# Attention with a position bias, then a gated FFN, on one core: another fixed issue order per engine

## The chip, the cores and the metric

One Trainium2 chip, of which the kernel uses one core. The metric is the device time of one execution in microseconds (us); the kernel before has a median of 652.33 us.

## The reference

The FFN's input is the attention's output; q, k and v are 4 x 8 x 576 x 64, w_in is 512 x 2048 and w_out 2048 x 512.

```python
def _attn_ref(q, k, v, w1, b1, w2):
    scores = scale * np.matmul(q, k.transpose(0, 1, 3, 2))
    rel = (pos[:, None] - pos[None, :]).astype(np.float32)
    psi_rel = np.log1p(np.abs(rel))
    psi_i = np.log1p(np.maximum(pos[:, None].astype(np.float32), 1.0))
    x = (psi_rel / psi_i)[..., None]
    h = np.maximum(x @ w1 + b1, 0.0)
    bias = h @ w2
    scores = scores + bias.transpose(2, 0, 1)[None, :, :, :]
    scores = scores - np.max(scores, axis=-1, keepdims=True)
    attn = np.exp(scores)
    attn = attn / (np.sum(attn, axis=-1, keepdims=True) + 1e-09)
    return np.matmul(attn, v).astype(np.float32)
...
x = np.ascontiguousarray(attn_out.transpose(0, 2, 1, 3)).reshape(B * S, H * D)
...
def _moe_ref(x, w_in, w_out):
    h = x @ w_in
    relu6 = np.clip(h + 3.0, 0.0, 6.0)
    g = h * relu6 / 6.0
    return (g @ w_out).astype(np.float32)
```

## The kernel before

**The bias table.** All heads and batches share one table of distances T. 36 groups of 16 positions are made. For a group, VectorE (DVE) or ScalarE (ACT) computes hidden units z (L1016, L1020; tiles `z_e` and `z_a`, used in turn), and TensorE (PE) multiplies them with w2 (`b_ps`: L1058 for the first 16 groups, L1037 for the later ones, which are written `bias_far`). ACT evicts (`bo`, L1076), and the table goes to HBM, from where later stages read it (`bias`, tile `bt`).

**The start.** DVE scales T by w1 in two halves (L1244: 636 columns, then 512), prepares b1 and w2 (L1247 to L1249) and clears a part of `z_a` (L1252), from which PE runs eight products of nothing but zeros (`w_ps`, L1255). Four small products `c_ps` (L1258) give the constant part of the bias, copied out at L1267.

**Attention** goes by units of two heads and a query tile. Scores `s_ps` are direct fp32 products for the first units (L683, with filler products of T before them, L680) and sums of three split products later (L703, of `qkh` from ACT, L557, and `qkl` from GpSimd, POOL, L564). DVE adds the bias and takes the maximum (L715), ACT takes exp (L726). The first units are transposed on PE (`t_ps`, L778 and L781) and evicted by ACT (`atf`, L784); the later ones are split into halves (`hl`, ACT L285 and DVE L302) and turned by a DMA (`at<-hl`). Products with V are `pv_ps` (L822, L833, L868).

**The FFN** takes blocks of 256 or 320 tokens: `h_ps` (L937) from `x` and `wi`, the gate on ACT (L927, L914), DVE (L920) and POOL (L916), then `o_ps` (L960) from `g` and `wo`; ACT evicts `ot` (L970). Before the first block its weights are split into high and low halves (L396 to L420, DVE L414, L417, L420, ACT L406), and DVE scales x (L1342, in `open_ffn`).

**Tile sizes on PE.** A product uses a part of the 128 x 128 array: h_ps, o_ps, t_ps and w_ps use 128*128 (rows * columns), b_ps and c_ps 128*32, s_ps 64*128 (one kind 128*128), pv_ps 128*64 or 64*64. Below, a switch is a matmul pass that has another tile size than the pass ahead of it on PE.

**The order.** The program is traced once. Then `ISSUE`, a table of numbers per engine (L36 on), gives the order in which each engine issues its instructions: the numbers are places in the traced sequence, and each instruction is made to follow the one before it in the list. After the end of a list the traced order goes on. The DMA queues of SP and POOL are in the table too.

```python
for name, seq in traced.items():
    order = []
    for run in ISSUE[name].split():
        lo, _, hi = run.partition("-")
        order.extend(range(int(lo), int(hi or lo) + 1))
    order.extend(range(len(order), len(seq)))
    for a, b in zip(order, order[1:]):
        tc.add_manual_dep(seq[b], seq[a].name, after, reason="order")
```

An engine so stands still at an instruction whose input is late, even if a later one in its list could run.

Of the kernel before, what the change touches and what calls it, by code (L numbers as in the profile page):

```python
# [37 lines left out]
0-1 3 2 23 4 6 15 18 5 20 7 10 8 22 25 11-12 9 13-14 17 31 16 19 21 26 24 27-28 30 33 29 32 38 34 47  # L38
36-37 35 51 54 40 48 39 43 59 42 50 57 55 52 41 60 44 49 45 62 46 63 56 53 58 65 67 69 68 64 61 66
76 70 75 73-74 78 77 80 79 71 83-84 82 72 81 86 85 87 89 91 90 94 92 99 88 97 95 101 93 98 96 102  # L40
100 103 109 108 106-107 112 111 110 113 104 114 117 105 121 116 120 119 122 124 118 115 130 123 132
127-129 134 133 135 131 126 125
""",
    "Pool": """
2-9 15 19 12 10 13 21 11 22 14 23 25-26 17 16 27 24 20 30 35 29 28 33 36 34 31 37 40 38-39 44 41 18
45 48 42 46-47 49 43 32 53 51 0 52 62 54 57 50 63 58 56 60 59 61 55 64 74 66 65 67-68 75 69 72 70-71
73 1 76 78 77 81 93 82 92 79-80 83-84 87 85 88 86 89 96 90-91 94 102-105 95 97-101 106-111 113-114
116-118 112 115 119 126-127 129-130 120-123 131 124-125 128 132 138-141 133-136 142 137 143-147
149-150 152-154 148 151 155 162-163 165-166 156-159 167 160-161 164 168 174-177 169-172 178 173
179-183 185-186 188-190 184 187 191 198-199 201-202 192-195 203 196-197 200 204 210-213 205-208 214  # L50
209 215-219 221-222 224-226 220 223 227 234-235 237-238 228-231 239 232-233 236 240-244 246 245
""",
    "Activation": """
0-1 3-4 7-8 5 12 11 6 9 15 13 16 19 2 14 20 17 24 21 28 10 18 22 25 29 26 32 36 27 37 23 33 30 41-42
31 34 38 46 45 40 35 39 43 50 58 44 47 52 51 59 55 74 54 62 48 56 61 65 53 66 63 57 49 67 64 70 68
75 71 60 80 72 69 73 81 77 76 84 78-79 82 86 88 83 90 85 87 89 92-94 96 99 91 102 95 97 101 100 108
104 103 106 109 107 111 113 110 137 146 112 114 117-118 105 98 115 119 121 116 120 123 151 125 122
124 126-127 129 132 152 128 173 131 157 134 130 139 142 140 138 147 158 165 135 141 133 148 153 144
136 166 149 154 174 159 145 160-161 175 167 162 168 201 155 143 150 163 176 169 180 186 177 181 156
192 188 182-183 187 164 189 205 171-172 193 184 178 194-195 206 179 190 216 202 196 198 207 185 191  # L60
204 199 218 208 219-221 213 215 222 214 223-224 217 203 200 225 170 209 226 238 232 210 233 211 231
227-228 197 229 234 212 244 266 264 235 230 236 241 258 242 280 250 237 243 247-248 239 274 253
256-257 240 254 245 259 265 246 249 260 293 262 255 263 251 272 267-268 261 270 269 271 273 276 275
281 285 278 277 282-283 291 279 284 286 292 252 290 302 294 297 287 295 304 298 289 296 288 303
305-306 300 313 307 323 299 336 301 309 308 310 312 311 314-315 319-321 318 324 322 330 316 329 333
325 334 331 317 326 328 332 345 327 343 335 340 350 341 337-338 342 347 339 346 355-356 351 344 361
352-353 357 354 358-359 365 348 372 349 367 374 366 368 371 360 369 394 362 370 364 382 389 363 379
373 375 377 376 383 378 384 390 386 392 380 406 388 385 381 393 391 395 408 397 396 399 407 387 432
398 400 423 409 401 411 417 410 418 402-403 424 404 413 405 415 414 416 420-421 425 419 430 437 422
431 412 427 426 438-439 433 429 428 434-435 440 459 444 467-468 436 450 445 441-442 451 443 446-448  # L70
457 452 449 462 458 453-454 463-464 456 455 476 465 484-485 471 466 460 472 461 474 479 475 469 480
470 481 473 482 486 483 477 487 478 496 507-508 489-490 494 502 500 488 495 501 491-493 497-498 503
505 499 513 506 504 509 514 510 526 511 518 512 538-539 515 519-520 524 516 531 533 517 522 525 532
521 523 528 527 529 534 536 530 544 537 535 540 545 541 557 542 549 543 565-566 546 550-551 555 547
560 562 548 553 556 561 552 554 563 567 564 558 568 559 576 584-585 572-574 579 581 575 571 580
569-570 582 586 583 577 587 578 596 607-608 589-590 594 600 602 588 595 601 591-593 598 597 603 605
613 599 606 614 604 609-610 626 611 615 638-639 618 612 619-620 616 624 631 633 622 625 617 632 621
623 627-629 634 636 644 630 637 645 635 640-641 657 642 646 665-666 649 643 650-651 647 655 660 662
653 656 648 661 652 654 663 667 664 668 658-659 676 684-685 672-674 679 681 675 671 680 669-670 682
686 683 687 677-678 696 707-708 689-690 694 700 702 688 695 701 691-693 698 697 703 705 713 699 706  # L80
# [12 lines left out]
68 60 58 63 61 70-71 73-74 72 75 67 82-84 87-88 91 79-80 92-93 89 85 94 109-110 90 96 122 100 81 104
97-99 101 108 119 102-103 123 105 112 115-116 113 117 114 121 126 125 129 118 127 133 124 106 128
131 107 132 111 137 143 120 130 153 138 135 144 139 172 175-177 173-174 136 134 141 149 180 142 155
150 148 146 183 147 145 140 313 154 152 184-185 163-164 181-182 151 188 191 160 158 189-190 165 157
166 156 161 167 192-193 162 159 200 203 199 178 201 168 204 169 186 202 170 205 179 210 213 197 194
209 214 195 198 187 215 211 206 216 222 212 223 225 207 226 196 227 224 230 218-219 221 208 231 451
228 233 239 232 217 234-235 171 236 245 237 220 248 238 249 269 259 251 246 229 241 252 240 242 247
258 243 253-254 257 256 261-262 274 273 293 275 263 284 260 266-268 277 276 265 278 281 270 250 279  # L100
244 289 255 280 264 286 272 296 285 294 282 287-288 283 297-298 290 314 291-292 316 315 330 306 308
295 299 326 317 302 301 300 320 335 305 307 304 309 318 303 311-312 331 319 310 327 336 328 324 321
323 329 325 322 332 338 342-343 339 334 346 333 341 350 348-349 344 337 347 360 354 340 355 345 356
351 361 359 357 368 365 362 352 364 372 358 453 369 371 363 379 366-367 370 376 378 387 375 271 377
# [1399 lines left out]
```

## Time and profile before

| what | before |
|---|---|
| time, three runs | 654.21, 652.02, 652.33 us; median 652.33 us |
| the profiled execution, its time and its span | 653.62 us, 651.5 us |
| granted clock of TensorE in it, as a share of full speed | 0.995 |
| TensorE busy | 625.5 us, 96% of the span, 5440 matmul passes |
| VectorE, ScalarE, GpSimd busy | 459.8, 504.7, 208.3 us |

The time of an execution is its span and 2.1 us around it. Busy times count an engine's instructions, without waits.

### The profile page before, as it was taken

How to read it: one execution, taken by the hardware profiler on the slowest of the kernel's cores; microseconds unless marked ns; L12 is line 12 of the kernel's file. 1: busy time of each engine (PE TensorE's matmuls, PEld its weight loads, DVE VectorE, ACT ScalarE, POOL GpSimd, SP SyncE). 2: the span in 40 equal slices, each digit the busy share in tenths (PEclk: the TensorE clock that was granted, in tenths of full speed). 3: DMA queues.
4: the chain of work that ended last, by engine and by line, in shares of the span. 5: the costliest groups of instructions: out<-in, count | busy, mean ns of one | idle time of the engine just before them, and what ended most of it. 6: DMA issues, size and time to landing. Idle time of an engine off the chain costs nothing.

```text
span 651.5 us, 14774 instructions
## 1 busy us (share of the span) xinstructions
PE 625.5 (96%) x5440; PEld 447.9 (69%) x5440; DVE 459.8 (71%) x1116; ACT 504.7 (77%) x993; POOL 208.3 (32%) x267
## 2 busy tenths in 40 slices
PE   6688998999999999999999999999999999999997
PEld 2225655666777777788888877777777777777775
DVE  4899999999858887676788667776677667821310
ACT  5898887999979989896799778976797678822620
POOL 0111115664223430452255125521444026300410
PEclk9889999999999999999999999999999999999999
DMA  8888788864679999999999999889878877640000
GB/s 278 317 322 298 283 310 318 308 232 140 163 205 247 215 274 194 264 251 234 257 259 248 203 209 180 176 177 205 173 142 187 181 168 139 113 81 21 1 12 31
DMA packets 176648, 130.57 MB, mean 200 GB/s; under 512 B 138304, under 2 KB 145728, under 8 KB 175552
## 3 DMA queue, kind: packets, MB, share of 16 engines
q1 hardware_dynamic: 166784, 114.14, 70.9%
q10 hardware_dynamic: 9792, 15.49, 8.5%
q8 instruction: 43, 0.70, 0.5%
q14 instruction: 29, 0.24, 0.1%
HBM read 77.54 MB, written 15.49 MB: 143 GB/s over the span
## 4 chain that ended last, share of the span: by engine, by line
PE 71%; DVE 4%; DMA 3%; ACT 1%; issue 0%; ACTq 0%; DVEq 0%; SPq 0%
PE o_ps L960 27%; PE h_ps L937 26%; PE s_ps L703 9%; PE pv_ps L868 6%; DMA at<-hl 2%; PE b_ps L1037 2%; DVE bt L715 1%; DMA wo<-in_w_out_dram 1%; DVE cu L420 1%; DVE cu L414 1%; ACT bt L726 0%; DVE wo L302 0%; PE pv_ps L822 0%; DVE cu L417 0%; ACT hl L285 0%
## 5 line engine op out<-in xcount | busy, mean ns | idle before, releaser
L937 PE MATMUL h_ps<-x,wi 128*128 128x256 f16 (+1 forms) x1536 | 205.7, 286 | 1.2 <-DVE x L1342 0.8
L960 PE MATMUL o_ps<-g,wo 128*128 128x256 f16 (+1 forms) x1536 | 198.8, 286 | 0.0
L937 PEld LDWEIGHTS <-wi 128*128 128x128 f16 x1536 | 146.6, 98 | 52.1 <-issue 15.8
L960 PEld LDWEIGHTS <-wo 128*128 128x128 f16 x1536 | 146.8, 98 | 46.4 <-issue 9.6
L916 POOL TENSOR_TENSOR g<-t,g 128x256 f16<-128x256 f32 (+1 forms) x128 | 105.0, 832 | 180.9 <-ACT g L914 173.9
L726 ACT ACTIVATE bt<-bt,sm 128x576 f32<-128x576 f32 x144 | 110.7, 770 | 31.0 <-DVE sm L715 30.6
L302 DVE SCALAR_TENSOR_TENSOR hl<-bt,sm,hl 128x576 f16<-128x576 f32 x112 | 95.2, 864 | 16.5 <-ACT hl L285 15.0
L285 ACT ACTIVATE hl<-bt,sm 128x576 f16<-128x576 f32 x112 | 84.0, 765 | 5.3 <-ACT bt L726 3.3
L920 DVE SCALAR_TENSOR_TENSOR t<-t,t,h_ps 128x320 f32<-128x320 f32 (+1 forms) x112 | 57.2, 516 | 40.2 <-ACT t L927 39.3
L564 POOL TENSOR_TENSOR qkl<-st,qkh 128x576 fp32r<-128x576 f32 (+2 forms) x48 | 53.1, 1124 | 90.3 <-ACT qkh L557 59.0
L914 ACT ACTIVATE g<-t 128x256 f16<-128x256 f32 (+1 forms) x128 | 54.9, 438 | 22.7 <-DVE t L920 22.3
L927 ACT ACTIVATE t<-h_ps,t,hr 128x320 f32<-128x320 f32 (+1 forms) x112 | 64.6, 586 | 8.4 <-PE h_ps L937 6.9
L715 DVE CUSTOM_DVE_ANT_0 bt<-s_ps,bt 128x576 f32<-128x576 f32 x88 | 64.8, 750 | 4.6 <-PE s_ps L703 4.4
L1016 DVE TENSOR_SCALAR z_e<-T,nbp 128x576 f32<-128x576 f32 (+17 forms) x76 | 36.5, 498 | 16.8 <-PE b_ps L1037 12.0
L734 DVE TENSOR_SCALAR sm<-sm 128x1 f32<-128x1 f32 x112 | 16.9, 151 | 44.0 <-ACT bt L726 43.7
L970 ACT ACTIVATE ot<-o_ps,os 128x256 f32<-128x256 f32 (+1 forms) x32 | 15.7, 491 | 38.4 <-PE o_ps L960 37.7
L1076 ACT ACTIVATE bo<-b_ps,cv_sb,isc 128x576 f32<-128x576 f32 (+36 forms) x60 | 36.7, 635 | 1.5 <-PE b_ps L1037 1.1
L715 DVE CUSTOM_DVE_ANT_0 bt<-s_ps,k 128x576 f32<-128x576 f32 x40 | 28.8, 752 | 5.9 <-PE s_ps L703 5.6
L407 POOL TENSOR_SCALAR w<-w 128x1024 f32<-128x1024 f32 x8 | 10.5, 1315 | 68.1 <-ACT wo L406 68.1
L868 PE MATMUL pv_ps<-at,vh 128*64 128x320 f16 (+1 forms) x432 | 32.0, 293 | 0.0
L1020 ACT ACTIVATE z_e<-T,bp 128x576 f32<-128x576 f32 (+17 forms) x36 | 24.9, 698 | 8.2 <-DVE bp L1247 3.4
L781 PE MATMUL t_ps<-eye_sb,bt 128*128 128x128 f32 x160 | 29.3, 280 | 1.1 <-ACT atf L784 0.5
(130 smaller groups left out, 845.0 us busy)
## 6 DMA issues: line engine op xcount, KB each, us to landing
bt<-bias SPq DMA_DIRECT2D x36, 576.0 KB, 5.6
w<-in_w_in_dram SPq DMA_DIRECT2D x8, 1024.0 KB, 6.6
vs<-in_vp_dram SPq DMA_DIRECT2D x24, 320.0 KB, 4.1
st<-in_qk_dram SPq DMA_DIRECT2D x16, 448.0 KB, 4.3
bias<-bo ACTq DMA_DIRECT2D x20, 295.5 KB, 4.4
wo<-in_w_out_dram SPq DMA_DIRECT2D x5, 1024.0 KB, 4.8
bias<-bo ACTq DMA_DIRECT2D x16, 288.0 KB, 4.3
bt<-bias SPq DMA_DIRECT2D x32, 144.0 KB, 3.3
```

What stands on the lines that cost most here:

```text
L285: nc.scalar.activation(out=out, in_=full, func=AF.Copy, scale=scale)
L302: nc.vector.scalar_tensor_tensor(out=out, in0=full, scalar=scale, in1=high, op0=ALU.mult, op1=ALU.subtract)
L703: nc.tensor.matmul(out=s_t[n + j][:, a, 0:HALF], lhsT=w[q], rhs=m[rows, cs], start=(k == 0), stop=(k == 2),)
L715: nc.vector.tensor_tensor_reduce(out=halves(bt), in0=ps, in1=halves(src), op0=ALU.add, op1=ALU.min, scale=-0.125, scalar=3.0e38, accum_out ...
L726: nc.scalar.activation(out=bt, in_=bt, func=AF.Exp, scale=-1.0, bias=sm[:, 0:1], accum_out=total)
L868: nc.tensor.matmul(out=ps[64 * s:64 * s + 64, 0:n], lhsT=w[:, 128 * c + 64 * s:128 * c + 64 * s + 64], rhs=at[:, c, s * n:(s + 1) * n], st ...
L914: nc.scalar.activation(out=g[:, 0], in_=uu, func=AF.Copy)
L916: e.tensor_sub(out=g[:, 1], in0=uu, in1=g[:, 0])
L920: nc.vector.scalar_tensor_tensor(out=t_t[f], in0=t_t[f], scalar=cols(f)[2], in1=h_t.pop(f)[:, 0:n], op0=ALU.min, op1=ALU.mult,)
L927: nc.scalar.activation(out=t_t[f], in_=h_t[f][:, 0:n], func=AF.Relu, scale=cols(f)[0], bias=cols(f)[1],)
L937: nc.tensor.matmul(out=h_t[f][:, 0:n], lhsT=wi[:, a, c, f * 128:(f + 1) * 128], rhs=x[:, e, c], start=(k == 0), stop=(k == 3 * KC - 1),)
L960: nc.tensor.matmul(out=ops[:, 0:n], lhsT=wo[:, a, f, e * 128:(e + 1) * 128], rhs=g_t[f][:, r], start=(f == 0 and a == 0 and r == 0), stop= ...
```

## The change

Only the table `ISSUE` differs: the products of PE, and the instructions of the other four engines' lists, are in another order. What is computed, the tiles and the buffers are the same. The table is 13 lines longer, so all lines after it stand 13 further down (L937 is L950).

```diff
 ISSUE = {
     "SP": """
-0-1 3 2 23 4 6 15 18 5 20 7 10 8 22 25 11-12 9 13-14 17 31 16 19 21 26 24 27-28 30 33 29 32 38 34 47
...
+0-1 3 2 7 4 15 18 6 20 5 8 22 10 23 25 11-12 9 14 13 17 31 16 19 21 26 24 27-28 33 30 29 47 32 34 36
...
```

Counted in the two orders, PE makes 276 switches before and 245 after. The places are given by the time at which the pass stands in the trace of before:

| stretch of the trace of before | switches before | after |
|---|---|---|
| up to the first h_ps (109.93 us) | 70 | 60 |
| from there to 302 us | 123 | 102 |
| 302 us to the end | 83 | 83 |

Of the 21 fewer after 109.93 us, 11 stand ahead of 160 us and 10 behind. From 302 us on PE's order is the same word for word; those of the other engines are the same or differ in which statistic is written first.

The first place is the start of PE's program. Before, `c_ps` stands between the products of zeros and ahead of the bias products `b_ps`:

```order
L1255 LDWEIGHTS z_a
L1255 MATMUL w_ps<-z_a 128x512
L1258 MATMUL c_ps<-b_sb,w_sb 32x1 x2
L1255 LDWEIGHTS z_a
L1255 MATMUL w_ps<-z_a 128x512
L1258 MATMUL c_ps<-b_sb,w_sb 32x1
L1058 MATMUL b_ps<-z_e,w_sb 32x288 x6
```

After, at the same place (the lines are L1268, L1271 and L1071 now):

```order
L1268 LDWEIGHTS z_a
L1268 MATMUL w_ps<-z_a 128x512
L1071 MATMUL b_ps<-z_e,w_sb 32x288
L1071 MATMUL b_ps<-z_a,w_sb 32x288
L1071 MATMUL b_ps<-z_e,w_sb 32x288 x3
L1271 MATMUL c_ps<-b_sb,w_sb 32x1
L1071 MATMUL b_ps<-z_e,w_sb 32x288 x2
L1271 MATMUL c_ps<-b_sb,w_sb 32x1 x2
```

The products of zeros are one run now, and the `c_ps` products stand among the `b_ps` products, which have their tile size.

The second place is the start of DVE's program, before:

```order
L1244 TENSOR_SCALAR T<-T,w_sb 128x636
L1240 MEMSET c_120 128x1
L1252 MEMSET z_a 128x576
L1247 TENSOR_SCALAR bp<-bp,b_sb 128x144
L1248 TENSOR_SCALAR nbp<-bp 128x144
L1016 TENSOR_SCALAR z_e<-T,nbp 128x576
L1016 TENSOR_SCALAR z_a<-T,nbp 128x576 x2
L1249 TENSOR_SCALAR w_sb<-w_sb 128x32
L1016 TENSOR_SCALAR z_e<-T,nbp 128x576 x2
L1238 MEMSET cv_sb 128x2
L1267 COPY cv_sb<-c_ps 32x1 x2
```

and after:

```order
L1265 MEMSET z_a 128x576
L1257 TENSOR_SCALAR T<-T,w_sb 128x636
L1253 MEMSET c_120 128x1
L1260 TENSOR_SCALAR bp<-bp,b_sb 128x144
L1261 TENSOR_SCALAR nbp<-bp 128x144
L1029 TENSOR_SCALAR z_a<-T,nbp 128x576
L1251 MEMSET cv_sb 128x2
L1029 TENSOR_SCALAR z_e<-T,nbp 128x576
L1262 TENSOR_SCALAR w_sb<-w_sb 128x32
L1029 TENSOR_SCALAR z_e<-T,nbp 128x576
L1029 TENSOR_SCALAR z_a<-T,nbp 128x576
L349 TENSOR_REDUCE vparts<-vf 128x1
```

The clearing of `z_a` is DVE's first instruction now, and one `z` fewer stands ahead of the scaling of w2. A reduction of V (L336, now L349) follows the fourth `z`, then comes the second half of T, and behind it the next `z_e` and the copies of `c_ps`. SP's list has the DMA of T's second half as its fifth and no longer as its twelfth.

The third place is on PE, where a unit of two scores is moved (with buffer numbers). Before, it stands at 271.1 us of the trace, inside FFN work:

```order
L937 LDWEIGHTS wi_95
L937 MATMUL h_ps_3518<-x_2436,wi_95 128x256
L703 MATMUL s_ps_3490<-qkh_3308 128x288
L703 MATMUL s_ps_3491<-qkh_3308 128x288
L703 MATMUL s_ps_3490<-qkh_3308 128x288
L703 MATMUL s_ps_3491<-qkh_3308 128x288
L703 MATMUL s_ps_3490<-qkl_3438,qkh_3308 128x288
```

After, it stands behind bias products that are at 261.2 us in the trace of before:

```order
L973 MATMUL o_ps_3209<-g_2823,wo_96 128x256
L1050 MATMUL b_ps_3351<-z_e_114,w2_sb_103 32x512 x4
L1050 MATMUL b_ps_3352<-z_e_114,w2_sb_103 32x64 x4
L716 MATMUL s_ps_3490<-qkh_3308 128x288
L716 MATMUL s_ps_3491<-qkh_3308 128x288
L716 MATMUL s_ps_3490<-qkh_3308 128x288
L716 MATMUL s_ps_3491<-qkh_3308 128x288
L716 MATMUL s_ps_3490<-qkl_3438,qkh_3308 128x288
```

The twelve score products of the unit stand ahead of the run of 73 `h_ps` passes and no longer inside FFN work, so one change of tile size is left out. On POOL the two parts of its `qkl_3438` keep their places, the second behind a part of the next unit's `qkl_3712`. On ACT the `qkh` that this next unit starts from now stands ahead of the `z_e` of these bias products and of one `hl`.

## Rows read from the trace of the kernel before

**Rows 1.** The page: busy time, share, instructions; the chain that ended last by engine.

```profile
PE 625.5 (96%) x5440; PEld 447.9 (69%) x5440; DVE 459.8 (71%) x1116; ACT 504.7 (77%) x993; POOL 208.3 (32%) x267
PE 71%; DVE 4%; DMA 3%; ACT 1%; issue 0%; ACTq 0%; DVEq 0%; SPq 0%
```

**Rows 2.** Windows: stretch, length, busy us (instructions) per engine, PEclk, DMA share, GB/s.

```profile
25.00:110.00 85.00, 75.08 (x534) 41.23 (x527) 80.65 (x169) 71.92 (x120) 19.18 (x16) 0.96 0.83 298
110.00:160.00 50.00, 48.61 (x390) 32.99 (x389) 49.15 (x115) 46.65 (x88) 30.07 (x27) 1.00 0.66 240
160.00:302.00 142.00, 141.41 (x1405) 107.48 (x1403) 109.10 (x287) 127.36 (x267) 48.94 (x67) 1.00 0.97 225
```

**Rows 3.** The chain that ended last, piece by piece, near 160 us: start, us, what.

```profile
159.54 0.76 DVE bt L715
...
160.36 0.44 PE t_ps L781 x2
```

**Rows 4.** Timeline of PE, 299 to 308 us: start, us, operation, tile, shape, passes.

```profile
299.87 0.53 PE L703 MATMUL s_ps<-qkh 64*128 64x288 f32 x4
300.23 0.43 PE L703 MATMUL s_ps<-qkl,qkh 64*128 64x288 f32 x4
300.50 0.43 PE L703 MATMUL s_ps<-qkh,qkl 64*128 64x288 f32 x4
300.86 2.79 PE L960 MATMUL o_ps<-g,wo 128*128 128x256 f16 x24
303.58 1.17 PE L868 MATMUL pv_ps<-at,vh 128*64 128x256 f16 x18
```

**Rows 5.** Timeline of PE at 117 us.

```profile
117.59 0.27 PE L781 MATMUL t_ps<-eye_sb,bt 128*128 128x128 f32 x1
117.70 0.71 PE L937 MATMUL h_ps<-x,wi 128*128 128x256 f16 x5
```

**Rows 6.** The page's costliest groups: mean ns of one weight load, second figure.

```profile
L960 PEld LDWEIGHTS <-wo 128*128 128x128 f16 x1536 | 146.8, 98 | 46.4 <-issue 9.6
```

**Rows 7.** Timeline of DVE, 0 to 17 us; in brackets idle time before, and its releaser.

```profile
3.87 0.55 DVE L1244 TENSOR_SCALAR T<-T,w_sb 128x636 f32<-128x636 f32 x1 [3.87 <-DMA w_sb<-in_w1c_dram]
...
4.49 0.54 DVE L1252 MEMSET z_a<- 128x576 uint32 x1
...
6.99 0.17 DVE L1249 TENSOR_SCALAR w_sb<-w_sb 128x32 f32<-128x32 f32 x1
...
11.62 0.52 DVE L1016 TENSOR_SCALAR z_e<-T,nbp 128x576 f32<-128x576 f32 x1 [4.03 <-PE c_ps L1258]
...
13.05 0.48 DVE L1244 TENSOR_SCALAR T<-T,w_sb 128x512 f32<-128x512 f32 x1
...
16.95 0.81 DVE L336 TENSOR_REDUCE vparts<-vf 128x1 f32<-128x640 f32 x1
```

**Rows 8.** Timeline of PE, 3 to 14 us.

```profile
5.09 3.17 PE L1255 MATMUL w_ps<-z_a 128*128 128x512 f16 x7 [5.09 <-DVE z_a L1252]
...
8.94 0.71 PE L1058 MATMUL b_ps<-z_e,w_sb 128*32 128x288 f32 x3
```

**Rows 9.** Waits of DVE, 0 to 112 us: total us, times, longest us.

```profile
DVE z_a L1016 <- PE b_ps L1058: 3.7, 4, 1.5
```

**Rows 10.** Waits of PE, 112 to 302 us, the longest of four rows.

```profile
PE h_ps L937 <- ACT ot L970: 0.5, 1, 0.5
```

**Rows 11.** Waits of PE, 0 to 112 us, the row of the first FFN block.

```profile
PE h_ps L937 <- DVE x L1342: 0.8, 1, 0.8
```

**Rows 12.** Windows at 24.5 us, columns as in Rows 2.

```profile
24.50:28.00 3.50, 3.27 (x21) 1.22 (x22) 2.97 (x4) 2.24 (x5) 0.00 (x0) 0.51 0.50 181
```

**Rows 13.** Timeline of PE, 262 to 272 us.

```profile
263.18 8.02 PE L937 MATMUL h_ps<-x,wi 128*128 128x256 f16 x71 [0.46 <-ACT ot L970]
271.13 0.53 PE L703 MATMUL s_ps<-qkh 64*128 64x288 f32 x4
```

**Rows 14.** Timeline of POOL, 240 to 272 us.

```profile
262.85 2.77 POOL L564 TENSOR_TENSOR qkl<-st,qkh 128x256 fp32r<-128x256 f32 x3 [15.96 <-DVE hl L302]
```

More of the change, by code (lines that the diff above doesn't have):

```diff
@@ new lines @@
+46 45 48 42 47 1 49 43 32 53 52 62 51 63 54 57 50 58 56 59-61 64-66 74 67-68 55 69 75 71 70 73 72 76
+78 77 81 93 82 80 92 84 83 79 86 88 87 89-91 103 85 94 104 95 102 98 97 99 105 100-101 110 108 96
+107 109 106 111 113-114 116-118 112 115 119 126-127 129-130 120-123 131 124-125 128 132 138-141
+133-136 142 137 143-147 149-150 152-154 148 151 155 162-163 165-166 156-159 167 160-161 164 168
+174-177 169-172 178 173 179-183 185-186 188-190 184 187 191 198-199 201-202 192-195 203 196-197 200
+204 210-213 205-208 214 209 215-219 221-222 224-226 220 223 227 234-235 237-238 228-231 239 232-233
@@ L52 @@
+236 240-244 246 245
 """,
     "Activation": """
[L54 to L68, printed above, removed]
@@ new lines @@
+504 514 505 500 510 513 509 511-512 516-518 515 519 523 521-522 527 532 525-526 531 502 520 524
+528-530 534-536 541 533 539-540 537 545 548 546-547 560 552-553 538 554 559 549-551 556-558 555
+564-566 561 563 572 562 570-571 567-568 575 578 576 573 577 582-583 590 569 584 589 574 579-581
+586-588 585 594-596 591 593 602 592 600-601 597-598 605 608 606 603 607 610-611 617 599 612 616 604
+609 613-615 619-621 626 618 624-625 630 622 627-629 632-633 639 634 623 638 631 635-637 641-643 648
+640 646-647 644 649 652 650-651 656-657 664 645 658 663 653-655 660-662 668-669 659 670 676 665-667
@@ new lines @@
+692 640-642 693 643 694 644 695-699 671-673 675 674 677 676 678-682 701-705 700 706-722 683-685
+723-728 745 686-687 746-750 741-744 729 731 733 735 737 739 730 769-776 732 734 939 736 738 740
+751-768 777-778 941 940 943 942 944-950 783-786 779-782 787-795 835 796-810 836 811 837 812-813
+838-839 814-816 840 817 841 818-819 842-844 820 845-846 821-822 847-848 823-824 849-850 825 851 826
+852 859-862 853-856 887 857-858 863 827 864 888 865-868 889 869-872 828 873 890 911-914 874 829 891
+830 892 875-876 831 893 832 894-896 877-878 833 897 879 898-899 880-881 900 834 901-902 882 903-909
@@ new lines @@
+951-954 883 910 915-919 884 920 885 955 921-923 886 924 956 925 957-958 926-929 959 930-931 960
+967-968 961 932 969 933-934 962-963 970 964-965 971 966 935-936 972 937 973 938 974 979-982 975 983
+995 976 984 996-997 985 998 986 999 987-988 977 989 1000 990 1001 991 978 992-994 1002 1007-1012
+1014 1013 1016 1015 1018 1017 1019-1022 1003-1004 1023 1035 1005 1024-1026 1036 1027 1006 1028
+1037-1041 1029 1042 1030-1031 1043 1032-1034 1047-1082 1044 1083-1085 1045 1086-1087 1046 1091
+1088-1089 1092 1090 1093 1115 1103-1108 1110 1109 1112 1111 1113-1114 1116-1119 1094 1120 1095
@@ new lines @@
+1121-1123 1132-1134 1124 1135 1096-1097 1136-1137 1125 1098 1126-1127 1138-1139 1099-1100 1128
+1144-1146 1140 1129 1147 1101 1130 1148-1150 1102 1151 1131 1141 1152 1142-1143 1168-1169 1171 1170
+1173 1172 1174-1177 1179 1178 1153 1156-1159 1154 1160 1155 1180-1183 1161 1184 1162 1185 1163-1166
+1186-1187 1167 1188 1196-1198 1189 1199-1200 1190 1201-1202 1191-1192 1203-1204 1193 1205 1194 1206
+1195 1207-1241 1252 1242-1244 1253 1245-1246 1254 1247-1249 1255-1257 1250-1251 1258 1264-1280 1259
@@ new lines @@
+1281-1294 1260 1295-1297 1261-1262 1298-1300 1263 1301-1303 1308-1315 1304-1307 1316-1321 1332-1333
+1335 1334 1336-1347 1322-1325 1348 1326-1327 1349-1352 1328 1353-1357 1329 1358-1365 1330-1331 1366
+1372-1403 1428-1433 1435 1434 1436-1437 1439 1438 1367-1371 1404 1440 1405-1408 1441 1409-1412
+1442-1443 1413 1444 1414 1445 1415-1419 1446 1420-1423 1447 1424-1425 1448-1461 1426 1462-1463
+1472-1475 1427 1476-1484 1464-1471 1485-1490 1496-1505 1507 1506 1508-1516 1491 1517-1520 1492
+1521-1523 1493 1524-1532 1494 1533 1495 1534 1540-1577 1579 1578 1581 1580 1583 1582 1584-1587
@@ new lines @@
+1773-1777 1792-1793 1778 1794-1798 1804-1805 1799 1806 1779 1800-1802 1816 1807-1808 1803 1809-1812
+1817-1822 1813 1823 1828-1829 1814 1830-1832 1824 1833 1815 1825 1852-1853 1834-1836 1826 1837
+1840-1845 1847 1846 1849 1848 1851 1850 1854-1855 1864 1856-1857 1838 1865 1839 1866 1827 1867
+1858-1859 1868 1860 1869-1870 1861 1871 1862 1872-1874 1863 1876-1903 1928-1931 1933 1932 1934-1939
+1875 1904-1918 1964 1919-1927 1965 1940 1966 1941-1943 1967-1968 1944 1969 1945-1950 1970 1951 1971
+1952-1956 1972-1973 1957 1974 1958-1963 1975-1987 2000-2007 1988-1989 1991 1990 1993 1992 1995 1994
@@ L170 @@
+1996-1999
 """,
```

193 lines of the change are left out of this document (89 added, 104 removed).

## The prediction

> **What bounds the kernel now.** I read the page first: TensorE (PE) is busy for 96% of the span, and it holds 71% of the chain that ended last [rows 1]. A shorter PE therefore counts, but not everywhere alike, so the windows come next. From 160 to 302 us PE is busy for 141.41 of 142 us, VectorE (DVE) for 109.10 and ScalarE (ACT) for 127.36. From 110 to 160 us it is DVE that never rests, 49.15 of 50 us, with PE at 48.61; from 25 to 110 us DVE has 80.65 of 85 us [rows 2]. The chain of work says the same: it is on DVE until the bias addition that starts at 159.54 us, and from 160.36 us it is on PE [rows 3]. Three stretches follow: up to 160 us what shortens DVE's own sequence pays, from 160 to 302 us what shortens PE's, and from 302 us on PE's order is unchanged.
>
> **What a switch costs.** The timeline of PE shows it between 299 and 308 us [rows 4]. Twenty-four o_ps passes take 2.79 us, and a single pass of that shape is 0.27 us long, so their starts are (2.79 - 0.27)/23 = 0.110 us apart. Twenty-four of these would be 2.63 us, but the next product, of another tile size, starts 303.58 - 300.86 = 2.72 us after the first: 0.09 us more. The score unit ahead of it gives the same: its middle four passes take 300.50 - 300.23 = 0.27 us from start to start, its last four, which end with the switch to o_ps, 300.86 - 300.50 = 0.36 us. A different operation is not dearer in itself: a transpose between h_ps passes has their tile size, and the next h_ps starts 117.70 - 117.59 = 0.11 us behind it [rows 5]. I take 0.09 us a switch; these rows leave 0.08 to 0.12.
>
> The Trainium skill, "TensorEngine Tiling (Array Packing)", section Key Properties, says that changing the tiling mode drains TensorE, and that a new tile alone does not; the rows agree. A rule speaks against the change: "TensorE: Matmul & The Clock Gate", Part 3, says that a weight load overlaps matmuls in flight only when it goes to another row group. By it, neighbours of one size on the same rows would pay for each load as well, and grouping them would bring nothing. The rows say otherwise: o_ps loads weights for every pass, 98 ns each [rows 6], on the same rows, and the passes are still 0.110 us apart, where load and pass one after the other would need 0.098 + 0.110 us.
>
> **The change part by part.**
>
> *From 160 to 302 us.* Ten switches fewer by 0.09 us = 0.9 us. PE does not wait for much here (the longest of four rows is 0.5 us [rows 10]), so the whole of it may pay; nothing of it pays if ACT, with 127.36 of 142 us busy, becomes late instead. Bounds 0 and 10 * 0.12 = 1.2 us; I take 0.9, since 14.6 us of idle time on ACT and 32.9 on DVE are free to follow a PE that is 0.6% shorter.
>
> *From 110 to 160 us.* Eleven switches fewer are 1.0 us of PE, but DVE sets the end of the stretch, and it can only be closed up by its own idle time, 50.00 - 49.15 = 0.85 us. Bounds 0 and 0.85; I take half, 0.4.
>
> *Up to 110 us.* Ten switches fewer, 0.9 us of PE, lie beside DVE, and pay only through the waits of DVE for PE, and through the start. At the start DVE stands still for 4.03 us, until 11.62 us, for PE [rows 7]. PE began w_ps at 5.09 us, because the clearing of z_a, 0.54 us, stood behind T, which waited 3.87 us for its DMA [rows 7, 8]; the first b_ps came at 8.94 us. Now the clearing waits for nothing, and the w_ps run can be over before the first z is made. Into the idle time of DVE two pieces are moved that stood behind it: half of T, 0.48 us, and a reduction of V, 0.81 us; the clearing lies in the time in which DVE waits for the DMA. With SP's list the half of T is loaded seven DMAs earlier, so it is there. What stood behind the 4.03 us becomes shorter by 0.48 + 0.81 = 1.3 us, and this is my term. The cover is the wait itself: if PE is so much earlier that the wait is under 1.3 us, the two pieces delay the next z by the rest, but then the wait was shortened by over 2.7 us and the sum is larger.
>
> The bounds: below, nothing, when the later waits of DVE for b_ps (3.7 us in four [rows 9]) only grow by what was won. Above, the whole 4.03 us: the w2 scaling ended at 7.16 us, 0.54 us of clearing and one z of 0.52 us are no longer ahead of it, so b_ps could begin at 6.1 us and not at 8.94, 2.8 us earlier, and 1.3 + 2.8 is the whole of it. I take 1.3, nearer to the lower half, because of the pace: seven w_ps passes of 512 columns take 3.17 us [rows 8], 0.45 us each, where the 256-column pace of [rows 4] would give 0.22. PE runs at half speed (1.2 GHz) there, although the granted clock reads full, and an earlier w_ps run followed by idle time may have to earn the full speed again with b_ps passes.
>
> At 109.93 us the first FFN block waits 0.8 us for DVE's scaling of x [rows 11]: from there on DVE's gain is passed on. Its instructions ahead of that scaling are the same ones, so nothing else is added to the chain.
>
> *Moved transfers.* The other moves on SP, POOL and ACT are costed at nothing: the core's transfers keep their number and size, and the work that covers them is PE's, 48.61 of 50 and 141.41 of 142 us. If that cover is gone, the wait shows on PE at the product that needs the transfer.
>
> *The moved score unit.* It stands 8.9 us earlier (from 271.13 us to about 262.3 us [rows 13]) and saves one switch, counted above. It needs a qkl part that is the second of three POOL instructions from 262.85 to 265.62 us [rows 14]. The qkh from which the first of these starts is made earlier on ACT, ahead of one z_e and one hl, so I expect no wait; the bound is the third rival.
>
> **The sum.** 1.3 + 0.4 + 0.9 = 2.6 us, 0.4%. The profiled execution took 653.62 us (a span of 651.5 and 2.1 around it) and would take 651.0; the median of the three runs is 652.33 us, from which it is 649.7 us. Bounds together: 0 and 4.0 + 0.85 + 1.2 = 6.1 us.
>
> **The rivals.** A measurement of this kernel can tell 0.3%, 2.0 us, from no change.
>
> *The gain is eaten.* PE saves its switches, and waits for DVE and ACT in their place: up to 160 us DVE is at 98%, and behind it ACT at 90% is released by PE and releases PE in turn. Only part of the start-up gain would stay, some 0.6 us: 651.7 us. For it speaks that DVE, not PE, sets the end of the stretch in which 11 of the 21 switches lie; against it, PE's few waits from 112 to 302 us.
>
> *A larger start.* b_ps begins 2.8 us earlier and the chain of DVE follows: 4.0 + 0.4 + 0.9 = 5.3 us, 647.0 us. For it speaks the 4.03 us wait, against it the half-speed passes.
>
> *The moved unit stalls PE.* PE takes its list in order, so twelve score products that wait for qkl hold 71 h_ps passes behind them, and the gate on ACT and DVE behind those. If POOL's three instructions keep their old times, the part comes at 264.3 to 265.6 us, and the h_ps run starts behind it and four last score passes (0.36 us) at up to 266.0 us rather than 263.18; 1.0 us of the unit is then no longer in the way at 271 us, so 1.8 us are lost against before: 654.1 us less the switches behind. It decides against the change if qkl is ready only after 266 us; 2 us more, which is less than another three POOL instructions of 2.77 us, give 656 us, slower.
>
> *The clock at the start.* A stretch at 24.5 us has a granted clock of 0.51 for 3.5 us with PE busy for 3.27 us [rows 12], twice as long as at full speed. If such a stretch falls behind the early w_ps run, it costs 1.6 us, and 1.3 becomes -0.3: 651.3 us.
>
> *A rule of the weight loads.* If grouping bought nothing on PE, the start alone would remain: 652.33 - 1.3 = 651.0 us. The spacing of 0.110 us with a load for every pass speaks against it. It is the rule of Part 3 above.
>
> That the change doesn't do what it says is no rival: the order has 31 switches fewer.
>
> **How the numbers follow.** The forecast has 0.55, with its own range of 648.5 to 650.8; the eaten gain 0.20, the larger start 0.10, the stalled unit 0.07, the clock 0.06, the weight loads 0.02. The range of 647.2 to 652.4 leaves out half of the larger start, the stalled unit and the worst of the eaten gain, together below 0.2. Faster by over 0.3% is under 650.4 us: the forecast but for its upper edge, 0.50, and the larger start, 0.10, make 0.60. Same takes that edge and the eaten, clock and weight cases, 0.32; slower, above 654.3 us, is the stalled unit and a little of chance, 0.08.
>
> **What would show each step.** The start: w_ps before 3 us, b_ps before 8 us, DVE's 4.03 us wait below 2 us, the scaling of x (109.5 us) about 1.3 us earlier. The stretch to 160 us: the first PE piece of the chain at 158.3 to 159 us. From there to 302 us: PE's passes that stood at 302 us come 2.6 us earlier, with no wait of PE in 112 to 302 us over about 0.6 us. A switch that is left must still cost 0.09 us. I am wrong if PE's waits in 112 to 302 us are over 1 us at any place, if h_ps behind the moved unit starts later than 263 us, or if the start-up gain is not there at 110 us.

## The result and the profile after

The changed kernel takes 657.87 us (median of 20 runs, 651.44 to 661.88); the kernel before took 652.26 us in the 20 runs beside them. The ratio is 1.007, with a 95% interval of 1.005 to 1.009: slower by 0.5 to 0.9%. The forecast was 649.7 us, and the range ended at 652.4.

The profiled execution is the fastest of the 20: 651.44 us, a span of 649.3 us, 2.2 us shorter than the profiled one of before. The page of it, busy time and chain, answers to [rows 1]:

```profile
PE 621.9 (96%) x5440; PEld 450.0 (69%) x5440; DVE 459.9 (71%) x1116; ACT 503.2 (78%) x993; POOL 209.2 (32%) x267
PE 76%; DVE 8%; DMA 2%; ACT 2%; issue 1%; ACTq 0%; SPq 0%
```

Its windows answer to [rows 2]:

```profile
25.00:110.00 85.00, 71.64 (x530) 42.41 (x529) 79.59 (x174) 72.14 (x122) 21.04 (x19) 0.98 0.90 322
110.00:160.00 50.00, 46.98 (x378) 32.19 (x375) 48.73 (x114) 45.54 (x87) 26.31 (x25) 1.00 0.57 200
160.00:302.00 142.00, 141.39 (x1417) 109.03 (x1416) 108.53 (x285) 126.40 (x266) 51.68 (x66) 1.00 0.94 230
```

TensorE (PE) is busy for less of the time ahead of 160 us, and waits for more of it. The start is as foreseen; these are PE's first products, and answer to [rows 8]:

```profile
1.52 3.60 PE L1268 MATMUL w_ps<-z_a 128*128 128x512 f16 x8 [1.52 <-DVE z_a L1265]
6.87 0.66 PE L1071 MATMUL b_ps<-z_e,w_sb 128*32 128x288 f32 x1 [1.75 <-ACT z_a L1033]
```

and these are DVE's pieces that were moved, which answer to [rows 7]:

```profile
8.57 0.82 DVE L349 TENSOR_REDUCE vparts<-vf 128x1 f32<-128x640 f32 x1 [1.00 <-DMA vf<-in_vp_dram]
9.31 0.48 DVE L1257 TENSOR_SCALAR T<-T,w_sb 128x512 f32<-128x512 f32 x1
10.11 0.52 DVE L1029 TENSOR_SCALAR z_e<-T,nbp 128x576 f32<-128x576 f32 x1 [0.32 <-PE b_ps L1071]
```

The bias products begin 2.1 us earlier, and the wait of 4.03 us is now 1.00 + 0.32 and later 1.06 us. The scaling of x comes at 104.50 us instead of 109.53. So the start of this one execution goes as predicted. It is not the typical one: it has one stretch at half clock, where the profiled execution of before has two. Even so most of its lead is gone by 160 us (in the second table below, 4.1 us at the 177th product and 0.8 us at the 716th). What differs in the others is the mean granted clock of TensorE: 0.997 in the profiled execution, 0.982 to 0.990 in 16 of the 20.

### The profile page after: what moved, and what is told of

Its sections match the earlier page's. It is cut to its first block, busy times and chain, and to the rows that moved or that the text cites. A ratio compares the mean times of both kernels' runs of the same rounds, so it can differ in the third digit from the quotient of the medians.

```text
span 649.3 us, 14751 instructions
## 1 busy us (share of the span) xinstructions
PE 621.9 (96%) x5440; PEld 450.0 (69%) x5440; DVE 459.9 (71%) x1116; ACT 503.2 (78%) x993; POOL 209.2 (32%) x267
## 4 chain that ended last, share of the span: by engine, by line
PE 76%; DVE 8%; DMA 2%; ACT 2%; issue 1%; ACTq 0%; SPq 0%
PE o_ps L973 29%; PE h_ps L950 27%; PE s_ps L716 9%; PE pv_ps L881 7%; PE b_ps L1050 3%; DVE bt L728 2%; DMA out_dram<-ot 1%; DVE cu L430 1%; DVE cu L427 1%; DMA wo<-in_w_out_dram 1%; DVE wi L315 1%; DVE cu L433 1%; DVE t L933 1%; DVE wo L315 0%; PE pv_ps L835 0%
## 5 line engine op out<-in xcount | busy, mean ns | idle before, releaser
L950 PE MATMUL h_ps<-x,wi 128*128 128x256 f16 (+1 forms) x1536 | 205.7, 287 | 0.8 <-ACT ot L983 0.6
L950 PEld LDWEIGHTS <-wi 128*128 128x128 f16 x1536 | 148.0, 98 | 48.9 <-issue 12.1
L577 POOL TENSOR_TENSOR qkl<-st,qkh 128x576 fp32r<-128x576 f32 (+2 forms) x48 | 54.4, 1151 | 86.1 <-ACT qkh L570 80.7
```

The costliest lines, as they stand in the source:

```text
L950: nc.tensor.matmul(out=h_t[f][:, 0:n], lhsT=wi[:, a, c, f * 128:(f + 1) * 128], rhs=x[:, e, c], start=(k == 0), stop=(k == 3 * KC - 1),)
```

## The experiments

All order experiments use one device: the first part of one kernel's order, up to a time in its own trace, on every engine; then the other kernel's order of all that is left. The diffs show the first place of PE's list at which a kernel leaves that of before. Each run took executions of before beside its own, and its ratio is against those. The clock in the table is the mean over the runs of a kernel of the granted clock of the whole span. "At full clock" is the mean time less 0.52 us for each 0.001 that the clock is below 1, the common slope of all these runs by least squares. The runs of before alone give the same: 650.5 us at 1.000 (17 runs), 651.6 at 0.997 (13), 652.9 at 0.995 (41), 654.6 at 0.992 (8). Two executions far off the rest (1241 us, and 667 us of before) are left out of the means; the medians hold them (without its one, after_again has 658.4 us).

| kernel (run) | order | median, us | mean clock | at full clock, us |
|---|---|---|---|---|
| before | before | 651.9 to 652.9 | 0.9959 | 650.2 |
| changed (first result, after_again) | changed | 657.9, 659.6 | 0.9889 | 651.9 |
| s14 | changed to 14 us | 650.82 | 0.9985 | 649.9 |
| s32 | changed to 32 us | 649.76 | 0.9964 | 648.4 |
| h_start | changed to 60 us | 654.67 | 0.9902 | 650.3 |
| m3260 | changed from 32 to 60 us | 655.44 | 0.9927 | 651.1 |
| h_rest | changed from 110 us | 653.38 | 0.9963 | 651.6 |
| rest_ot2 | the same, two ot buffers | 652.79 | 0.9955 | 650.3 |
| after_ot2 | changed, two ot buffers | 656.85 | 0.9888 | 650.9 |
| b160 | changed from 160 us, two ot buffers | 652.00 | 0.9956 | 649.8 |
| best | changed to 32 and from 160 us, two ot buffers | 649.06 | 0.9962 | 647.3 |

A second table, worked out from the starts of the same products in each trace, gives the time by which all of the first 177, 716 and 2011 products of before's order have started (60.1, 160.0 and 302.0 us there):

| trace | 177 | 716 | 2011 | 716 to 2011 |
|---|---|---|---|---|
| before, before_again | 60.1, 58.0 | 160.0, 158.1 | 302.0, 300.0 | 142.0, 141.9 |
| s32, h_start, m3260 | 57.1, 57.5, 57.3 | 156.9, 158.9, 158.3 | 298.6, 300.4, 300.2 | 141.8, 141.5, 141.9 |
| changed, after_again | 56.0, 60.4 | 159.2, 166.7 | 300.0, 309.0 | 140.9, 142.3 |
| h_rest, rest_ot2 | 60.1, 60.1 | 160.5, 162.2 | 303.4, 303.3 | 142.9, 141.1 |
| after_ot2, b160, best | 58.9, 59.8, 57.9 | 164.5, 159.5, 157.7 | 304.8, 300.2, 298.3 | 140.4, 140.7, 140.6 |

**The two kernels again.** No edit.

> The changed kernel once more, for the profile of another execution: the profiled one of before took 651.44 us, the fastest of 20, whose median is 657.87 us, and the mean granted clock of the others is lower (0.982 to 1.000, for 0.997). Theory 1 (the clock): an execution of 655 to 660 us has the same order and the same waits, but one or more further stretches at half clock of some 3.5 us and more, together 10 to 20 us long, that lie where TensorE has pauses, ahead of 110 us or around the first FFN block; behind 160 us the windows have the busy time of the first profile. Theory 2 (waits): the clock is much the same by stretches, and TensorE's waits on DVE and ACT between 110 and 302 us have grown by 4 us or more.

> The kernel before once more, for the profile of another execution: its times lie between 650.67 and 655.66 us. Theory 1: stretches at half clock, together under 8 us, in the first 110 us, at other places or of other lengths than in the first profile, and the same windows behind 160 us within 0.3 us. Theory 2: the same stretches as in the first profile.

after_again was 660.89 us in its profiled execution, with a clock of 0.989. Its windows show where; PEclk is the third figure from the end:

```profile
24.00:27.00 3.00, 3.00 (x32) 1.71 (x24) 1.69 (x5) 1.99 (x4) 0.00 (x0) 0.61 0.32 56
...
30.00:33.00 3.00, 2.56 (x24) 1.22 (x26) 2.73 (x6) 2.19 (x4) 0.20 (x1) 0.50 0.99 396
...
66.00:69.00 3.00, 3.00 (x11) 1.49 (x9) 1.36 (x5) 2.25 (x3) 0.00 (x0) 0.50 1.04 427
...
160.00:302.00 142.00, 139.39 (x1388) 106.13 (x1387) 108.92 (x293) 127.27 (x266) 47.22 (x61) 1.00 0.92 222
```

There are three places at the half clock (1.2 GHz) ahead of 75 us, none of which the first profile has (it has one, from 102 to 107 us). At the last, PE is busy for the whole window with 11 passes, and VectorE (DVE) and ScalarE (ACT) wait in its place: DVE is busy for 1.36 of 3 us. Each begins in or behind a pause of PE. The timeline of PE at the third:

```profile
64.85 0.80 PE L791 MATMUL t_ps<-eye_sb 128*128 128x128 f32 x2 [2.25 <-DVE sm L728]
65.44 1.27 PE L794 MATMUL t_ps<-eye_sb,bt 128*128 128x128 f32 x5
66.51 1.17 PE L693 MATMUL s_ps<-T,eye_sb 128*128 128x288 f32 x2
```

The other profiles agree: in the second table's twelve traces and that of s14, each of the 27 half-clock stretches ahead of the last product starts inside a pause of PE of 1.3 to 2.6 us, or within 1.7 us of its end. A pause is not enough, though: these traces have 70 of 1.3 us or more, and one of 2.33 us at 43 us in the first profile of the changed kernel was followed by full speed. Theory 1 holds for these stretches. Of the 9.4 us that this execution takes longer than the first profiled one, 7.5 us are lost by the 716th product; at 0.52 us for 0.001 of clock the lower clock explains 4.2 us. So theory 2 has a share, and behind 160 us too, since the waits of PE for ot are 2.0 us here and 0.6 us there. before_again took 650.99 us with a single half-clock stretch (36 us) where the first profile had two.

**The changed start alone, and how far.**

The edit, in PE's list from its 8th place on (the same in the three):

```diff
-8 9 7 10 12 13 14 15 16 17
+7 12 20 13 14 15 8 16 17 9
```

> The changed kernel's order up to 60 us of its trace, and from there the order of the kernel before. Theory 1a (the new start makes the slow clock): slower than before by 3 to 6 us, with the changed kernel's lower mean clock. Theory 1b (the clock falls because of the order behind 60 us): within 1.5 us of before or up to 1.3 us faster, with the clock of before. Theory 2 says as 1b.

> The changed kernel's order up to 14 us of its trace, from there the order of before. It has the early run of zero products, the two pieces moved on VectorE and the pause of 1.7 us ahead of the first bias products, but not the changed kernel's order of bias products behind. Theory 1 with the cause in the first 14 us: mean clock 0.990 as in h_start (order up to 60 us), median 654 to 656 us. Theory 1 with the cause behind 14 us (the pauses of 1.3 to 2.4 us between 20 and 60 us): mean clock 0.995 to 0.997 as before, median 650 to 652.5 us.

> The same with the changed kernel's order up to 32 us. If the clock is lost by the pauses between 20 and 32 us, mean clock about 0.990 to 0.993 and a median of 653 to 655 us; if by those between 32 and 60 us, the clock and time of s14.

Theory 1a held for h_start: the clock fell to 0.990, the median rose by 2.8 us. But s14 and s32, which stop earlier, keep the clock of before (s14 has a higher one) and are faster, with ratios of 0.9962 (0.9943 to 0.9981) and 0.9963 (0.9942 to 0.9983). The pauses up to 32 us, on which the expectation of s32 turned, cost nothing. The loss is in the order from 32 to 60 us. This rests on the means over twelve executions, not on the places in one: of the four half-clock stretches in h_start's profile two begin ahead of 32 us (22.4 and 29.2 us), where s32 has the same order.

**The order from 32 to 60 us alone.**

PE's list from its 84th place on:

```diff
-82 83 84 85 86 87 88 89 90 92
+84 82 83 85 86 87 88 89 90 91
```

> The order of before up to 32 us, the changed kernel's between 32 and 60 us, then before's. If the pauses of the changed order between 32 and 60 us cost the clock by themselves, mean clock 0.990 to 0.993 and a median of 655 to 657 us; if only together with the changed first 32 us, clock 0.995 to 0.997 and 652 to 653.5 us.

655.44 us, a ratio of 1.0053 (1.0028 to 1.0077), clock 0.9927: by itself it costs 3.1 us, and about half of the clock that it costs behind the changed start (0.0032 below before, h_start 0.0062 below s32). What it does shows in PE's timeline. Before:

```profile
42.30 0.76 PE L683 MATMUL s_ps<-qk 64*128 64x288 f32 x4
42.98 0.68 PE L1058 MATMUL b_ps<-z_e,w_sb 128*32 128x288 f32 x4
43.59 0.75 PE L683 MATMUL s_ps<-qk 64*128 64x288 f32 x2
44.27 0.67 PE L1058 MATMUL b_ps<-z_e,w_sb 128*32 128x288 f32 x2
44.87 0.75 PE L683 MATMUL s_ps<-qk 64*128 64x288 f32 x2
45.55 1.16 PE L1058 MATMUL b_ps<-z_e,w_sb 128*32 128x288 f32 x10
```

In m3260 the scores stand together, and so do the bias products:

```profile
39.55 1.24 PE L684 MATMUL s_ps<-qk 64*128 64x288 f32 x6
40.73 1.18 PE L1059 MATMUL b_ps<-z_e,w_sb 128*32 128x288 f32 x16
44.64 1.18 PE L1059 MATMUL b_ps<-z_a,w_sb 128*32 128x288 f32 x16 [2.74 <-ACT z_e L1021]
...
56.42 1.25 PE L684 MATMUL s_ps<-qk 64*128 64x288 f32 x8
59.64 0.95 PE L681 MATMUL s_ps<-T,eye_sb 128*128 128x288 f32 x2 [1.97 <-ACT atf L785]
60.52 1.33 PE L684 MATMUL s_ps<-qk 64*128 64x288 f32 x4
```

Before, the score products filled the time in which DVE and ACT made the next z, and PE has no pause over 0.6 us between 40 and 60 us. Grouped, the products of one size are over at once and a pause of 2.74 us follows. The pause of 1.97 us has a forerunner before, of 1.26 us:

```profile
61.63 0.75 PE L680 MATMUL s_ps<-T,eye_sb 128*128 128x288 f32 x2 [1.26 <-ACT atf L784]
```

It ends in a half-clock stretch, in the windows of m3260:

```profile
57.00:60.00 3.00, 1.03 (x8) 0.50 (x4) 1.76 (x2) 2.13 (x3) 0.86 (x1) 1.00 1.02 364
60.00:63.00 3.00, 3.00 (x11) 1.72 (x10) 2.96 (x9) 3.00 (x6) 0.27 (x1) 0.51 1.06 428
```

That stretch alone does not tell the orders apart: s14 and rest_ot2, which have before's order there, have one at the same product, behind pauses of 1.51 and 1.45 us. And the profiled execution of m3260, the fastest of its twelve, is level with before_again at the same clock (0.997): 651.05 and 650.99 us, the 716th product at 158.3 and 158.1 us. So the twelve executions show that this order costs time and clock. That it does so through its pauses is supported by a count: behind the first product PE pauses for 1.3 us or more 2 to 5 times in each of the eight profiles with before's order from 32 to 60 us, and 6 to 9 times in each of the five with the changed one. No run takes away the pauses alone, so more than that is not shown.

The switches that were left out here, 0.1 us each, were those at which PE went over to work that it could do.

**Filling the pauses.** Extra products on PE, at the head of each early bias group.

```diff
+        for _ in range(2):
+            nc.tensor.matmul(out=pss[0][:, 0:HALF], lhsT=eye_sb, rhs=T[:, 640:640 + HALF])
         for a in range(2):
             for k, z in enumerate(zs):
```

> The changed kernel with two extra fp32 products (T by the unit matrix, 288 columns, some 0.5 us each) at the head of each of the 16 early bias groups, into the bank that the group then overwrites: 16 us more TensorE work, most of it inside pauses of 0.3 to 2.4 us. Theory 1 (the slow executions come from half-clock stretches behind those pauses): the mean clock is 0.995 or higher in nearly all executions, fewer than two half-clock stretches ahead of 75 us, and the median falls from 658 to 650 to 654 us, with a spread under 4 us. Rival (the slow executions come from late DMAs or engines, and the clock only follows): the median stays at 656 us or more, or rises with the added work.

> The kernel before with the same filler products. Theory 1: its two half-clock stretches (24.5 and 38 us of its profile) go as well, 1 to 3 us faster than before, if the fillers do not delay the bias products; its spread (650 to 655 us) shrinks. Rival: slower by up to 2 us, since TensorE has more to do.

667.25 and 666.62 us, slower by 14 us, with clocks of 0.9937 and 0.9952. The clock of the changed kernel rose (0.9889 without), that of before did not, and the time expected was missed by far: of the 16 us of added work 9 came on top of the changed kernel's time and 14 on top of before's. The bias groups have no room for it. So whether filled pauses alone would win the time back was not shown.

**The order behind 110 us, and one buffer.**

PE's list of h_rest from its 392nd place on:

```diff
-372 392 377 373 374 378 408 379 409 380
+408 372 377 378 392 373 374 379 409 410
```

> The order of the kernel before up to 110 us of its trace, and from there the changed kernel's. Theory 1a: 1 to 1.5 us faster than before, since the 21 switches saved behind 110 us stay and the start of before keeps its clock. Theory 1b with the cause ahead of 110 us: the same. Theory 2 (waits behind 110 us): 3 to 6 us slower than before, as the changed kernel is.

With the clock of before it is 1.5 us slower (ratio 1.0025, 1.0007 to 1.0043), though it has 21 switches fewer. Theory 1a had forecast a gain; theory 2's sign is right, with half of its lower bound. Up to the 716th product it lost 0.6 us on before, from there to the 2011th 0.9 us. ACT shows why in the second stretch. The waits of ACT of h_rest, 160 to 302 us, against none of this kind before:

```profile
ACT ot L981 <- DMA out_dram<-ot: 4.3, 2, 2.4
```

and ACT and PE at the first of the two:

```profile
190.60 0.47 ACT L981 ACTIVATE ot<-o_ps,os 128x256 f32<-128x256 f32 x1 [2.42 <-DMA out_dram<-ot]
191.12 0.49 PE L948 MATMUL h_ps<-x,wi 128*128 128x256 f16 x3 [0.53 <-ACT ot L981]
```

ot has one buffer, so it can't be written before the last one is stored. In before two o_ps were done at 184.37 and 188.34 us and the store had landed at 187.86; in h_rest they are 3.56 us apart (185.61, 189.17), and the store lands at 190.51. That the two are 0.4 us closer is the smaller part. The store is issued at 186.15 us in both, and takes 1.7 us in before and 4.4 us in h_rest; at 1.7 us it would have been in time. What differs around it is the transfers: the DMA share, the figure before the last, is 0.09 in before (first line) and 1.11 in h_rest.

```profile
186.00:187.00 1.00, 1.00 (x12) 0.90 (x10) 1.00 (x4) 1.00 (x3) 0.00 (x0) 1.00 0.09 33
186.00:187.00 1.00, 1.00 (x15) 0.54 (x12) 0.00 (x0) 1.00 (x3) 0.00 (x0) 1.00 1.11 369
```

The other edit is the second buffer:

```diff
-            ot = f_p.tile([128, gw], F32, tag="o", bufs=1, name="ot")[:, 0:n]
+            ot = f_p.tile([128, gw], F32, tag="o", bufs=2, name="ot")[:, 0:n]
```

> The order of the kernel before up to 110 us, then the changed kernel's, as in the run h_rest, with two buffers for the FFN's output tile ot in place of one. Theory 3 (behind 160 us the switches saved are given back because ScalarE waits for the store of the last ot, 4.3 us in two waits, and TensorE's h_ps for ScalarE, 1.9 us): the two waits for the store are gone, 160 to 302 us takes 141.0 to 141.5 us in place of 142.9, and the median falls from 653.4 to about 651.9 us. Rival (ScalarE would be late there anyway): the stretch stays above 142.3 us.

> The whole changed order with two buffers for ot. Theory 3 (the single buffer costs 1.3 us) and theory 1 (the start costs the clock) together: the mean clock stays at 0.988 to 0.990 and the median falls only by 1 to 1.5 us, to about 656.5 us. Rival (the buffer is the main cause): 653 us or less.

As theory 3 said: the waits are gone and the stretch takes 141.1 us in place of 142.9. The median fell by only 0.6 us (1.3 at full clock), short of the 1.5 expected. In the whole changed order the buffer brings about 1 us and the clock stays at 0.9888: the buffer is not the main cause.

**The price of a switch.** In before's order the last instruction of one size and the first of the next change places, which makes two switches more. The first of the 30 places of more_sw, and the first of the 18 of sw_pv:

```diff
-2229 2230
+2230 2229
...
-2347 2348
+2348 2347
```

> The kernel before with 60 more changes of tile size: at 30 borders between 320 and 417 us the last instruction of one tile size and the first of the next change places. Forecast of the prediction: 0.09 us each (0.08 to 0.12), so 5.4 us slower (4.8 to 7.2), all of it between 320 and 420 us. Rival (a switch costs nothing that other engines do not hide, or half): under 3 us.

> The kernel before with 36 more changes of tile size behind 334 us, at 18 borders between pv_ps and h_ps or o_ps only, where no pass of a pair is parted from its partner. At the 0.09 us of the prediction: 3.2 us slower (2.9 to 4.3). Rival (0.148 us, the figure of the run with 60 more, holds for every switch): 5.3 us.

8.8 and 4.2 us slower in the medians. The traces are clearer, since the granted clock is full in them behind 302 us. The products that stand between 320 and 420 us in before's trace take 100.0 to 100.1 us in every trace that has them in this order, and 110.9 us in more_sw; those between 334 and 600 us take 266.0 to 266.1 us, and 272.0 us in sw_pv. That is 10.9 us for 60 switches and 6.1 us for 36: 0.18 and 0.17 us for a switch, against the forecast. The timeline of sw_pv shows an error in the design:

```profile
347.53 0.84 PE L872 MATMUL pv_ps<-at,vl 128*64 128x320 f16 x9
348.31 0.28 PE L941 MATMUL h_ps<-x,wi 128*128 128x256 f16 x1
348.52 0.32 PE L872 MATMUL pv_ps<-at,vl 128*64 128x320 f16 x1
348.77 0.28 PE L941 MATMUL h_ps<-x,wi 128*128 128x256 f16 x1
```

and these are the same products before:

```profile
349.72 0.85 PE L868 MATMUL pv_ps<-at,vl 128*64 128x320 f16 x10
350.50 0.28 PE L937 MATMUL h_ps<-x,wi 128*128 128x256 f16 x1
```

Before, ten pv_ps and the switch took 0.78 us. pv_ps passes go two at a time, on the two column halves, so the expectation that no pair is parted was wrong: nine take as long as ten. The swap costs 0.78 + 0.21 + 0.25 us less 0.78 and a pass of h_ps of 0.11, 0.35 us; of these 0.14 are the pass without a partner, which leaves 0.21 for two switches, 0.11 each. By this the 18 swaps of sw_pv make 6.3 us, and its trace has 6.1. s_ps passes go by twos as well, on the two row halves. In more_sw the two swaps around twelve of them take 0.73 us; less 0.13 for the parted pairs that is 0.15 us a switch.

**What can be kept.**

> The order of before up to 160 us, then the changed kernel's, with two buffers for ot. If the ten switches saved behind 160 us bring 0.9 us once the wait for ot is gone, and the loss of rest_ot2 lies ahead of 160 us: 651.5 us, 160 to 302 us in 141.0 us. If the switches bring nothing: 652.5 us, 142 us.

> The changed kernel's order up to 32 us, before's up to 160 us, then the changed kernel's, with two buffers for ot: 2 us from the start (s32) and 0.9 us from the switches behind 160 us, 649 to 649.8 us, faster than both kernels, with the clock of s32 (0.996). If gains at the start are taken back by waits further on: 650.5 us or more.

PE's list of b160 from its 717th place on; best has the 8th place of s32 as well, and both have bufs=2 for ot:

```diff
-683 684 721 685 686 722 723 741 742 743
+721 722 683 684 685 723 724 725 726 727
```

b160 has 140.7 us from the 716th to the 2011th product, 1.2 us less than before's trace (142.0; 141.5 to 142.4 in the eight traces with before's order there). The buffer alone is not what wins it: PE waits for ot for 0.5 us of the stretch in before, and in b160 for a z_e for 0.6. But its median of 652.0 us (0.9998, 0.9979 to 1.0017) can't be told from before. best takes 649.06 us, as was expected, a ratio of 0.9962 (0.9941 to 0.9984): faster than both kernels by 3.3 and 8.8 us.

## Why the prediction was wrong

- **The step that failed** is *Up to 110 us*: ten switches fewer "lie beside DVE, and pay only through the waits of DVE for PE, and through the start", with a bound of nothing below. Its lower bound was wrong. Between 32 and 60 us the grouping took away work that filled PE's waits for z. m3260 shows the price of that alone (3.1 us between medians, of which about 1.7 through the clock, 0.0032 * 520), and s32 against h_start gives 4.9 us (5.9 when each is set against the runs of before beside it). In the whole change the clock, by the common slope, accounts for 0.0070 * 520 = 3.6 us of the 5.3 us between the means. That the regrouping lowers the clock through PE's pauses is argued from their number (6 to 9 of 1.3 us or more, for 2 to 5) and not shown by a run of its own.
- **The rival of the clock** had the right mechanism and the wrong place, size and chance. It was looked for behind the early w_ps run, once, at 1.6 us. The place is seldom the one: s14 has the highest clock of all, 0.9985, though in the profile of best a half-clock stretch does begin at 7.8 us, behind the pause that follows the early w_ps run. Most stretches come further on and several in one execution, and [rows 12] had shown one in before.
- **The start** was right in size, and in part by luck: 1.3 us forecast, s14 1.6 and s32 2.0 us less than before in the means (650.7 and 650.3 against 652.3). But 0.0026 * 520 = 1.4 us of s14's gain go with its higher clock, on which the prediction did not count, and at full clock only 0.3 us are left; s32, with the clock of before, keeps 1.8 us. So the gain takes the order up to 32 us and not the first 14 us alone.
- **From 110 to 160 us** the forecast was 0.4 us of gain. From the 391st to the 716th product (109.9 to 160.0 us in before's trace) h_rest takes 51.1 us and rest_ot2 51.2; the ten traces that keep before's order there take 49.3 to 50.4. DVE is busy in both orders (it stands idle for 1.1 us between 104 and 164 us in h_rest, as before), so it may be that work was moved ahead of the release of PE; this was not tried, and the cause stays open. The whole changed order loses more from the 177th to the 716th product, 103 to 106 us for 100, of which half-clock stretches explain a part only.
- **From 160 to 302 us** the 0.9 us are there, 1.2 us in b160 and best, when ot has two buffers. With one they are given back: the rival *The gain is eaten*, at a place that the prediction did not name. It set [rows 10], h_ps waiting for ot, aside as small, and *Moved transfers* put the new order of the transfers at nothing, while a store that took 1.7 us took 4.4.
- **The price of a switch**, 0.09 us (0.08 to 0.12), was measured as 0.11 beside pv_ps and 0.15 beside s_ps. [rows 4] had the rest: the first four s_ps passes behind the switch take 0.36 us to the next, the middle four 0.27. The drain that "TensorEngine Tiling (Array Packing)" of the Trainium skill states in Key Properties is borne out; the rule of "TensorE: Matmul & The Clock Gate", Part 3, by which grouping would bring nothing, is not, since the stretch from 160 to 302 us does get shorter.
- **The moved unit** did not stall PE: the run of h_ps behind it has no wait for it in the profile after.
- The profile of one execution misled twice. The clock of an order is spread over its executions, and neither the first profile of before (two stretches) nor of the changed kernel (one) says how often they come: at 0.0026 of clock for a stretch the mean clocks make 1.6 and 4.3 of them an execution.

Open is what makes the clock fall behind one pause and not behind another of the same length, and where m3260's loss at full clock (0.9 us) lies, since its profiled execution does not show it.

## What to carry to other kernels

Count a saved switch at its 0.1 us only where the engine has no wait; where it waits, ask first whether the switch is the place at which it goes over to work that is ready. A new order should be timed over many executions, with the granted clock beside each time, before its one profile is believed. When an order moves transfers, look at the buffers that results leave through: a store that landed just in time before, from a single buffer, is the next wait.

## What the runs showed that was not expected

- Executions of one kernel differ by whole half-clock stretches, at 0.52 us of time for 0.001 of mean clock over all kernels here. A stretch as in [rows 12], 3.5 us at 0.51, lowers the mean by 0.0026 and so costs about 1.4 us on average, most of the 1.7 us that PE loses in it. That DVE and ACT wait for PE there holds for some: in after_again they are busy for 1.36 and 2.25 of the 3 us from 66 us, in m3260's stretch for 2.96 and 3.00.
- The w_ps run at the start is at half speed in both kernels (seven 512-column passes in 3.17 us before, eight in 3.60 after), whether it begins at 5.09 or 1.52 us, and the profile's clock row reads full there. When the speed rises differs by execution. The first b_ps passes at full speed (0.41 us long in place of 0.69) come at about 11 us in the first profiles of both kernels, but at 8.7 us in before_again and from the first one, at 6.8 us, in h_start, which has the changed start.
- A pv_ps pass without a partner on the other column half takes the time of a pair, 0.14 us, more than the 0.11 us of the switch beside it.
